# The last re/im swap of a long convolution: eight GpSimd copies in place of four DMAs, and the list order that goes with it

## The chip, the cores and the metric

One core of one Trainium2 chip. The metric is the device time of one launch in microseconds (us). The kernel before took 248.62 us in the median of two runs (248.44 and 248.81).

## What is computed

`x` has 2048 rows of 512 channels, in bfloat16. Two layers follow each other twice, with the same weights: a gated long convolution (A) and an MLP (B).

```python
# A: q = layernorm(x), k and v are given
k_shift = sum over t of 4 taps: k[s - 3 + t] * shift_k[:, 3 - t]
kv = k_shift * v
y  = irfft(rfft(kv padded to 2S) * rfft(ssm_k padded to 2S))[:S] + kv * ssm_D
x  = x + layernorm(x) * y
# B
h  = gelu(layernorm(layernorm(x)) @ w1 + b1)
x  = x + h @ w2 + b2
```

The convolution's result `y` depends on k, v, shift_k, ssm_k and ssm_D alone, and not on x. So it is computed once and used by both A layers.

## The kernel before, in words

**The convolution.** The 2048 time steps are cut into two halves of 1024. Each half is carried to the frequency side by matmuls with tables, and multiplied there. On the frequency side a number is complex. A tile is 128 partitions by 8192 columns, and a column group of 128 belongs to eight channels. The two groups of 64 partitions of a tile hold the two parts (re and im) of each number. One such group can be multiplied elementwise with another tile only as it lies; for the cross terms of a complex product a second copy of the tile is needed, with its two groups of 64 partitions swapped. That copy is the "swap" of this case.

The steps of one half, with their lines in the kernel before:

- `turn_h` (L563, matmuls at L571) turns the filter ssm_k. `turn_k` (L577, L589) and `taps` (L596, L609) make kv of the first half on TensorE, and `shift` (L703) makes that of the second half on VectorE.
- `stage1` (L617, matmuls at L630) and `stage2` (L635, matmuls at L644) transform it. Eight matmul groups of each make one tile. Each group of PSUM is moved to SBUF by `evac` (L539): an ACTIVATE on ScalarE (L544) or a copy on VectorE (L545), 128x1024 numbers at a time.
- The swaps: `swap_v` (L661) with pool=1 copies on GpSimd, 64 partitions at a time, viewed as 32-bit words (L667). The filter's first half is swapped so (C3 to C4), and the filter's second part too (C6 to C4). `swap` (L649) copies the second half's kv (C5 to C1) by four SBUF to SBUF DMAs of 512 KB, two issued by SyncE and two by ScalarE (through `dma`, L525).
- The products, elementwise on VectorE (`tt`, L534). Those of the second half, L870 and L871, go over four pieces g of 2048 columns: m = C5\*C3, C6 += m, then m = C1\*C3, C4 += m. The second pair needs the swapped tile C1.
- `inverse1` (L674, matmuls at L682, eight groups, two for each piece g) and `inverse2` (L688, L697) go back to time and give y.

**The MLP blocks.** Eight blocks of 512 rows (L962: `for L, b in ...`, counted k = 0 to 7): the A layer's norm and gating, then the layernorms, then the MLP. k = 0 to 3 use the first half's y, k = 4 to 7 the second half's. Statistics are VectorE's (L894 to L901), but the power -0.5 is GpSimd's (L902), and VectorE (L904) or ScalarE goes on with it. `norm` (L936) runs on ScalarE (L941) or VectorE (L942). The normed rows are transposed by DMA from SyncE's queue (L999), except in block 0 (on TensorE, L1007). The first MLP matmul is L1022, the gelu on ScalarE L1027, the second matmul L1042, and VectorE adds its result to x (L1046). A block is 44 matmuls of 512 columns at L1022 and 44 at L1042.

**What sets the order.** Nothing is run in the order in which it is written. Each operation is recorded with a cost and with what it reads and writes. `schedule` (L188) is a list scheduler: it walks over a model of the five engines, and picks for each engine the ready operation with the highest priority. The priority is the longest path behind an operation, plus a boost for its stage, plus an offset from a table that gives some operations, by number, a nudge (L1055). It also decides which engine, ScalarE or VectorE, empties a PSUM group, and which PSUM banks are used. `sync` (L320) sets the semaphore waits, and each engine then runs its list strictly in order. So a table entry can move any operation on any engine. A GpSimd operation waits in addition for the one before it on GpSimd.

Of the kernel before, what the change touches and what calls it, by code (L numbers as in the profile page):

```python
# [418 lines left out]
                getattr(block, e)(body)  # L419


WF, SPL, NA1, NDX, KP, KM, SG, PG, PSW, PLN, END, SPS, ST4, IA, SWA, PSH, BPE, TQ = 8, 1, 0, 64, 2, 0, 1, 1, 1, 0, 1, (0, 4), 0, 0, 0, 1, (), ()
S, D, FF = 2048, 512, 1376
B = 1024
EPS = 1e-5
# [39 lines left out]
def bass_interleave_layers__ssm_conv_h3__mixer_channel_mlp__prompt_kernel(  # L465
# [7 lines left out]
    def A(p0, n, off, *dims):  # L473
        return bass.AP(ar, p0 * AR + off, [[AR, n]] + [list(d) for d in dims])
# [16 lines left out]
    def place(n):  # L491
        o = pos[0]
        pos[0] += n
        return o
# [5 lines left out]
    C1, C3, C4, C5, C6 = (place(8192) for _ in range(5))  # L500
# [134 lines left out]
    def stage2(s, dst0, hf, g, dg0=0, nd=64, engs=None):  # L635

        tl = Tile(cv[hf], 0, hi[hf])
        nk = 1024 // nd
        ins = [(i, A(0, 128, R_S2 + (nk * g + i) * 128, [1, 128]), A(0, 128, s + (nk * g + i) * 64 + dg0, [1, nd]))
               for i in range(nk)]  # L640

        def f(e):
            for i, w, m in ins:
                r = e.matmul(Q(tl, 0, 128, i * nd, [1, nd]), w, m, start=True, stop=True)  # L644
            return r
        P.op(PE, f, nk * 29.0, reads=[x for y in ins for x in y[1:]], tile=tl, ni=2 * nk)
        evac(A(0, 128, dst0 + dg0 * 128 + nk * g, [128, nd], [1, nk]), lambda: Q(tl, 0, 128, 0, [1, nd], [nd, nk]), tl, engs)

    def swap(dst0, src0, dg0=0, nd=64):  # L649
        out = []  # L650
        for h in range(2):
            s = A(64 * h, 64, src0 + dg0 * 128, [1, nd * 128])
            out.append(dma(A(64 - 64 * h, 64, dst0 + dg0 * 128, [1, nd * 128]), s, nd * 37500, reads=[s], eng=(ACT if SWA else SP, ACT)[h]))
        return out

    def W32(p0, n, off, nd, nk):

        whole = bass.AP(ar, 0, [[AR, 128], [1, AR]]).bitcast(mybir.dt.int32)
        return bass.AP(whole.tensor, (p0 * AR + off) // 2, [[AR // 2, n], [64, nd], [1, nk // 2]] if nk < 128 else [[AR // 2, n], [1, nd * nk // 2]])

    def swap_v(dst0, src0, k0, nk, dg0=0, nd=64, pool=0):  # L661
        for h in range(2):
            i = A(64 * h, 64, src0 + dg0 * 128 + k0, [128, nd], [1, nk])
            o = A(64 - 64 * h, 64, dst0 + dg0 * 128 + k0, [128, nd], [1, nk])
            if pool:
                i2, o2 = W32(64 * h, 64, src0 + dg0 * 128 + k0, nd, nk), W32(64 - 64 * h, 64, dst0 + dg0 * 128 + k0, nd, nk)
                P.op(POOL, lambda e, i2=i2, o2=o2: e.tensor_copy(o2, i2), 1050.0, reads=[i], writes=[o])  # L667
            else:
                P.op(DVE, lambda e, i=i, o=o: e.tensor_copy(o, i), 710.0, reads=[i], writes=[o])
# [110 lines left out]
    for b in range(4):  # L780
        o, i = A(0, 128, R_DG + b * 512, [128, 4], [1, 128]), A(0, 128, R_ID, [0, 4], [1, 128])
# [73 lines left out]
            tt(o, A(0, 128, C5 + g, [1, n]), o, ALU.mult, 0.522 * n + 75.0)  # L855
    for g in range(8):
        stage2(C1, C5, 1, g)
    for i in range(2):
        swap(C1, C5, 32 * i, 32)
    if IA:  # L860
        for g in range(4):
# [101 lines left out]
    for L, b in [(0, 0), (0, 1), (1, 0), (1, 1), (0, 2), (0, 3), (1, 2), (1, 3)]:  # L963
# [89 lines left out]
                o = (b // 2) * B * 512 + (s % 8 - 1) * 512  # L1053
                outs.append(dma(dr(out, o, [8 * 512, 128], [1, 1024]), src, 1 << 18, reads=[src], writes=[]))
    P.schedule({  # L1055
        4: -2859500, 5: -2332800, 6: -1286000, 7: -1568900, 9: -2780000, 10: -3423500, 11: -4494400, 12: -7936200,
        13: -3456200, 14: -2083000, 15: -1086600, 17: -1246300, 18: -6727400, 49: 623300, 51: 1120500, 53: 397800,
        55: 878200, 57: 134800, 59: 357300, 61: 272900, 63: 442100, 65: 724800, 67: 1864700, 71: 1802700,
        73: 1680700, 75: 701900, 77: 2335500, 79: 3094300, 85: -855100, 87: -630300, 89: 139200, 122: -790700,
        140: 2949200, 142: 2930700, 148: 1114000, 149: -654400, 150: 2949300, 152: 2948900, 176: -1426600,  # L1060
        177: 1935700, 178: -1855200, 179: 1936500, 208: 1864200, 211: 1900900, 212: 2323700, 214: 1229900,
        215: 415700, 216: 1737900, 218: 2034800, 241: 274700, 252: -1863500, 254: -2126300, 261: 1300, 262: 1300,
        273: 692100, 274: 458400, 297: -395900, 323: -399300, 337: 1307700, 338: -581200, 371: 253000, 376: -62100,
        392: -327100, 404: -326700, 408: -517800, 419: -335200, 422: -237100, 430: -638000, 447: 389200, 448: 63500,
        449: -913400, 469: -1612800, 475: -1234900, 477: -724700, 481: -1965000, 483: -2062800, 485: -2047800,
        487: -1764900, 488: -752200, 495: -1158700, 500: -183700, 507: 501700, 508: -2594600, 525: -1427300,
        548: -4015000, 552: -130700, 564: -122800, 570: -595600, 572: -40300, 574: -359400, 576: -197300,
        580: -29700, 592: -1116400, 675: -2740700, 682: 2523700, 683: 850400, 772: -120300, 817: -3898900,
        819: -3017300, 821: -4122100, 823: -492500, 825: -4399400, 827: -4740300, 829: -3454600, 831: -2091700,
        833: -663100, 835: -1261600, 837: -1188500, 845: 1101200, 931: 187700, 1018: 1087200, 1019: 549100})  # L1070
    P.sync()
    P.emit(outs)

# [27 lines left out]
```

## Time and profile before

| what | value |
|---|---|
| two runs | 248.44 and 248.81 us, median 248.62 |
| the profiled execution | 248.81 us, of which the span is 246.8 us |
| granted TensorE clock | 1.00 |
| busy: TensorE, VectorE, ScalarE, GpSimd | 237.3, 185.0, 164.4, 49.7 us |
| TensorE's idle time with a cause, after the first 12 us | 5.2 us, the last of it at 118.7 us |
| GpSimd's swap copies (L667) | 16, median 1.037 us, longest 2.982 us |
| the four swap DMAs | 512 KB each, 7.5 us to landing (SyncE's), 8.9 us (ScalarE's) |
| last matmul group of `stage2` ends | 118.2 us |

Times in the views are microseconds from the start of the span. A row of the timeline gives start, length, engine, line, operation, operands, how often, and in brackets the idle time before it with what ended it. "PE" is TensorE, "DVE" VectorE, "ACT" ScalarE, "POOL" GpSimd; "SPq" and "ACTq" are the instruction queues of SyncE and ScalarE when they issue DMAs. Neighbouring equal instructions are merged in one row.

### The profile page before, as it was taken

What the parts mean: (1) busy time and instruction counts of PE and PEld (TensorE: products, weight loads), DVE (VectorE), ACT (ScalarE), POOL (GpSimd) and SP (SyncE); (2) the same over time, 40 slices, a digit from 0 to 9 for tenths busy, and PEclk for the clock granted to TensorE, in tenths of its full rate; (3) what the DMA queues carried; (4) which work ended last, traced back from release to release, by engine and by line L of the source; (5) the groups of instructions that cost most, each with busy time, mean ns of one, the idle gap of its engine ahead of it and who ended that gap; (6) DMA issues with size and microseconds to landing.
All of it is one profiled execution on the core that took longest, in us unless ns stands there. A gap on an engine that the chain in (4) does not pass through costs nothing.

```text
span 246.8 us, 5684 instructions
## 1 busy us (share of the span) xinstructions
PE 237.3 (96%) x2448; PEld 146.1 (59%) x2448; DVE 185.0 (75%) x353; ACT 164.4 (67%) x223; POOL 49.7 (20%) x48
## 2 busy tenths in 40 slices
PE   7999988899899999999899999999999999999995
PEld 4687778896687644455445647447844444444543
DVE  3579868999999998899989996699156866942012
ACT  3386779999999945868665589738914823733710
POOL 0000573000404396401304031122001111020000
PEclk9999999999999999999999999999999999999999
DMA  6999990613001440003590510033400030033002
GB/s 164 386 426 415 401 319 13 238 25 151 3 3 21 66 170 3 0 3 65 122 238 4 137 36 0 3 85 86 86 2 0 1 78 10 0 65 106 3 11 74
DMA packets 22097, 24.79 MB, mean 100 GB/s; under 512 B 15955, under 2 KB 17848, under 8 KB 20664
## 3 DMA queue, kind: packets, MB, share of 16 engines
q1 hardware_dynamic: 21752, 23.34, 30.5%
q10 hardware_dynamic: 320, 1.09, 1.9%
q8 instruction: 19, 0.31, 0.5%
q14 instruction: 6, 0.05, 0.1%
HBM read 16.56 MB, written 2.10 MB: 76 GB/s over the span
## 4 chain that ended last, share of the span: by engine, by line
PE 74%; ACT 14%; POOL 7%; DVE 2%; issue 1%; DMA 1%; POOLq 0%
PE ps L1042 28%; PE ps L1022 27%; ACT ar L544 12%; POOL ar L667 5%; PE ps L644 4%; PE ps L630 3%; PE ps L682 3%; PE ps L571 2%; POOL sm L902 2%; PE ps L609 1%; PE ps L697 1%; PE ps L768 1%; PE ps L762 1%; DMA ar<-ar 1%; DVE ar L534 1%
## 5 line engine op out<-in xcount | busy, mean ns | idle before, releaser
L544 ACT ACTIVATE ar<-ps 128x1024 bf16<-128x1024 f32 (+2 forms) x89 | 86.0, 1052 | 21.5 <-PE ps L630 8.6
L1027 ACT ACTIVATE ar<-ps,sm 128x512 bf16<-128x512 f32 (+3 forms) x110 | 63.5, 607 | 39.1 <-PE ps L1022 38.8
L534 DVE TENSOR_TENSOR ar<-ar 128x2048 bf16<-128x2048 bf16 (+2 forms) x76 | 77.9, 1054 | 5.1 <-ACT ar L544 2.8
L1022 PE MATMUL ps<-ar 128*128 128x512 bf16 (+3 forms) x440 | 80.9, 337 | 0.4 <-DMA ar<-ar 0.4
L1042 PE MATMUL ps<-ar 128*128 128x512 bf16 (+2 forms) x363 | 80.6, 373 | 0.3 <-ACT ar L1027 0.3
L1022 PEld LDWEIGHTS ps<-ar 128*128 128x128 bf16 (+1 forms) x440 | 42.9, 100 | 33.2 <-DMA ar<-ar 0.8
L1042 PEld LDWEIGHTS ps<-ar 128*128 128x128 bf16 (+1 forms) x363 | 34.6, 98 | 38.2 <-ACT ar L1027 0.9
L902 POOL TENSOR_TENSOR sm<-sm 128x2 f32<-128x2 f32 (+1 forms) x24 | 28.8, 1199 | 127.9 <-DVE sm L901 127.1
L1046 DVE TENSOR_TENSOR ar<-ar,ps 128x512 bf16<-128x512 bf16 (+1 forms) x33 | 21.6, 667 | 33.7 <-PE ps L1042 33.5
L894 DVE BATCH_NORM_STATS2 sm<-ar 128x6 f32<-128x512 bf16 x64 | 42.3, 683 | 0.3
L941 ACT ACTIVATE ar<-ar,sm 128x512 bf16<-128x512 bf16 x23 | 18.0, 808 | 9.1 <-DVE sm L904 5.6
L630 PE MATMUL ps<-ar 128*64 128x128 bf16 x640 | 22.1, 221 | 1.7 <-ACT ar L544 1.4
L667 POOL COPY ar<-ar 64x1024 int32<-64x1024 int32 x16 | 19.4, 1212 | 19.4 <-DVE ar L545 12.5
L630 PEld LDWEIGHTS ps<-ar 128*64 128x64 bf16 x640 | 18.5, 110 | 7.3 <-ACT ar L544 2.8
L644 PE MATMUL ps<-ar 128*128 128x64 bf16 x512 | 18.9, 193 | 2.9 <-ACT ar L544 1.3
L644 PEld LDWEIGHTS ps<-ar 128*128 128x128 bf16 x512 | 16.9, 98 | 6.6 <-ACT ar L544 3.1
L942 DVE TENSOR_SCALAR ar<-ar,sm 128x512 bf16<-128x512 bf16 x41 | 15.7, 410 | 1.6 <-POOL sm L902 1.1
L682 PEld LDWEIGHTS ps<-ar 128*128 128x128 bf16 x256 | 14.7, 98 | 1.4
L682 PE MATMUL ps<-ar 128*128 128x128 bf16 x256 | 15.5, 219 | 0.0
L545 DVE CAST ar<-ps 128x1024 bf16<-128x1024 f32 x9 | 10.8, 1219 | 2.4 <-PE ps L644 1.3
L896 DVE BATCH_NORM_AGGREGATE sm<-sm 128x2 f32<-128x6 f32 x64 | 10.3, 174 | 0.3
L904 DVE SCALAR_TENSOR_TENSOR sm<-sm 128x2 f32<-128x2 f32 (+1 forms) x21 | 3.6, 175 | 6.8 <-POOL sm L902 6.8
(33 smaller groups left out, 72.5 us busy)
## 6 DMA issues: line engine op xcount, KB each, us to landing
ar<-tab_s SPq DMA_DIRECT2D x4, 1024.0 KB, 18.1
ar<-in_A_ssm_k_dram SPq DMA_DIRECT2D x4, 512.0 KB, 6.9
ar<-in_A_q_dram SPq DMA_DIRECT2D x2, 1024.0 KB, 6.6
ar<-in_A_v_dram SPq DMA_DIRECT2D x2, 1024.0 KB, 8.9
out_dram<-ar SPq DMA_DIRECT2D x7, 256.0 KB, 2.4
ar<-in_A_k_dram SPq DMA_DIRECT2D x1, 1408.0 KB, 7.7
ar<-in_B_w_dram SPq DMA_DIRECT2D x1, 1376.0 KB, 22.1
ar<-in_B_w_dram SPq DMA_DIRECT2D x1, 1280.0 KB, 23.9
```

Of the source, the lines that this page charges most:

```text
L534: return P.op(eng, lambda e: e.tensor_tensor(o, a, b, op), dur, reads=[a, b], writes=[o])
L544: return e.activation(dst, src(), AF.Copy)
L630: r = e.matmul(Q(tl, 64 * ri, 64, i * 128, [1, 128]), w, m, start=j == 0, stop=j == len(terms) - 1)
L644: r = e.matmul(Q(tl, 0, 128, i * nd, [1, nd]), w, m, start=True, stop=True)
L667: P.op(POOL, lambda e, i2=i2, o2=o2: e.tensor_copy(o2, i2), 1050.0, reads=[i], writes=[o])
L682: r = e.matmul(Q(tl, 0, 128, i * 128, [1, 128]), w, m, start=j == 0, stop=j == len(pp) - 1)
L894: P.op(DVE, lambda e, st=st, x=x: e.bn_stats(st, x), 630.0, reads=[x], writes=[st])
L902: P.op(POOL, lambda e: e.tensor_tensor(r, v, h, ALU.pow), 1200.0, reads=[v, h], writes=[r])
L1022: r = e.matmul(Q(tl, 0, rows, 0, [1, nt]), w, m, start=dk == 0, stop=dk == 3)
L1027: P.op(ACT, lambda e, dst=dst, tl=tl, rows=rows, bias=bias, nt=nt: e.activation(dst, Q(tl, 0, rows, 0, [1, nt]), AF.Gelu_apprx_tanh, bias= ...
L1042: r = e.matmul(Q(tl, 0, 128, 0, [1, n]), ins[fc][0], ins[fc][1], start=fc == 0, stop=fc == 10)
L1046: P.op(DVE, lambda e, x=x, tl=tl, n=nc2: e.tensor_tensor(x, x, Q(tl, 0, 128, 0, [1, n]), ALU.add), 85.0 + nc2 * 1.055, reads=[x], writes=[ ...
```

## The change

Two things change. The second half's swap C5 to C1 is done by `swap_v` on GpSimd: four pieces of 2048 columns, two copies of 64 partitions each, in place of the four DMAs. And the table of offsets is another one: 126 entries in place of 112, on operations whose numbers behind the swap have moved by four.

```diff
-WF, SPL, ..., SWA, PSH, BPE, TQ = 8, 1, ..., 0, 1, (), ()
+WF, SPL, ..., SWA, PSH, BPE, TQ, PSX = 8, 1, ..., 0, 1, (), (), 1
...
     for g in range(8):
         stage2(C1, C5, 1, g)
-    for i in range(2):
+    for g in range(4 if PSX else 0):
+        swap_v(C1, C5, 0, 128, 16 * g, 16, pool=1)
+    for i in range(0 if PSX else 2):
         swap(C1, C5, 32 * i, 32)
...
     P.schedule({
-        4: -2859500, 5: -2332800, 6: -1286000, 7: -1568900, 9: -2780000, 10: -3423500, 11: -4494400, 12: -7936200,
...
+        4: -692700, 5: -476200, 6: -284700, 7: -137700, 9: -1381500, 10: -1285800, 13: -1222000, 14: -1491500,
...
```

Both kernels can be built, so the lists of all engines are known, though not their times. In the list after, the amount of work is the same on TensorE (2448 matmuls of the same shapes). These differences bear on what follows:

- Loads on SyncE: two of the four `stage2` tables go ahead of the load of v, the other two come right behind it, and the table of `inverse1` goes behind w1.
- In the first part (up to the second `turn_h`) VectorE empties 12 of the 32 large PSUM groups of `stage1` and `stage2` and not 9, and ScalarE 20 and not 23; of the eight smaller groups of `turn_k`, ScalarE empties six and not three. The first power on GpSimd stands ahead of the first-half copies and not behind six of them.
- Further on, four norms of block 2 stand together on ScalarE, where two were on ScalarE and two on VectorE.
- Behind the last `stage2` group TensorE has 44 matmuls of L1022 and 22 of L1042 (block 2) ahead of the first `inverse1` group, where it had 44 and 26; the eight `inverse1` groups and the four `inverse2` groups stand one by one between MLP matmuls, where some stood in pairs.
- GpSimd's list there is: one copy, the power of block 3's first norm, seven copies, the two powers of block 3's second norm.
- SyncE's two and ScalarE's two swap DMAs are gone from their lists.

## The prediction

> **What bounds the kernel now.** I read the page first, then TensorE's timeline, then the chain of waits, then the other engines' timelines where the chain leaves TensorE.
>
> ```profile
> span 246.8 us, 5684 instructions
> PE 237.3 (96%) x2448; PEld 146.1 (59%) x2448; DVE 185.0 (75%) x353; ACT 164.4 (67%) x223; POOL 49.7 (20%) x48
> ```
>
> TensorE is the bound, but not everywhere. Its timeline shows where it loses time; the last idle bracket of the whole run is this:
>
> ```profile
> 117.71 0.64 PE L644 MATMUL ps<-ar 128*128 128x64 bf16 x16 [0.31 <-DVE ar L1046]
> 118.74 6.42 PE L1022 MATMUL ps<-ar 128*128 128x512 bf16 x28 [0.39 <-DMA ar<-ar]
> ...
> 134.07 1.06 PE L682 MATMUL ps<-ar 128*128 128x128 bf16 x16
> ```
>
> From 118.74 to 244.12 us TensorE runs without a gap (44 matmuls of 512 columns in 9.51 us, 0.216 each). So whatever comes earlier ahead of the last L644 group (end 118.2, call it T) is won at the end, and whatever stalls TensorE behind T is lost. Between 42.3 and 70 us the chain lies on ScalarE (L544, 16.49 and 8.56 us), which empties PSUM without a pause while VectorE is full too. Ahead of that everyone waits for everyone:
>
> ```profile
> 26.99 6.52 POOL L667 COPY ar<-ar 64x1024 int32<-64x1024 int32 x6 [12.49 <-DVE ar L545]
> 33.60 2.10 POOL L902 TENSOR_TENSOR sm<-sm 128x4 f32<-128x4 f32 x2
> ...
> 34.65 0.41 DVE L942 TENSOR_SCALAR ar<-ar,sm 128x512 bf16<-128x512 bf16 x1 [1.06 <-POOL sm L902]
> ```
>
> A power (L902) stands behind six copies, and VectorE behind the power. The swap that is replaced, and what VectorE does beside it:
>
> ```profile
> 119.44 1.18 SPq L525 DMA_DIRECT2D ar<-ar  x2
> ...
> 119.82 2.07 ACTq L525 DMA_DIRECT2D ar<-ar  x2
> 121.94 2.42 ACT L1027 ACTIVATE ar<-ps,sm 128x512 bf16<-128x512 f32 x4 [1.44 <-PE ps L1022]
> ...
> 125.09 0.69 DVE L534 TENSOR_TENSOR ar<-ar 128x1024 bf16<-128x1024 bf16 x1 [1.00 <-ACT ar L941]
> ...
> 130.76 1.20 DVE L534 TENSOR_TENSOR ar<-ar 128x2048 bf16<-128x2048 bf16 x1
> 132.00 1.22 DVE L534 TENSOR_TENSOR ar<-ar 128x2048 bf16<-128x2048 bf16 x1
> ```
>
> Last, how copies and products treat each other, from the chain and VectorE's timeline (a copy alone takes 1.04):
>
> ```profile
> 91.07 2.43 DVE L534 TENSOR_TENSOR ar<-ar 128x4096 bf16<-128x4096 bf16 x1
> ...
> 91.42 2.99 POOL ar L667
> 94.46 1.04 POOL ar L667
> ```
>
> The copy that starts under a product makes no headway until the product ends (2.99 = 1.04 + 1.95). The product that starts 0.29 ahead of the end of the copy before it takes 2.43 and not 2.29; another (85.83, 1.33 and not 1.22) lost 0.11 under 0.26 of a copy.
>
> **The change, step by step.** All sums are against the profiled execution (248.81 us, span 246.8); the median is 0.19 below it, and I carry the differences over to 248.62.
>
> 1. Up to 42 us: the list. I followed the lists after by hand from 12.4 us, with 0.91 for a large emptying on ScalarE back to back, 1.14 on VectorE, 0.6 for L894, 1.85 for a `taps` group, 0.5 for an L630 or L644 group, 1.04 a copy. ScalarE sheds three large groups and takes three small ones (3 x 0.91 - 3 x 0.53 = 1.1 less), VectorE takes 2.3 more but no longer waits 1.06 for the power, which goes ahead of the copies. Emptying of the second `turn_h` then starts at about 40.4 (42.26 before), the products on VectorE at 40.25 (42.24): -1.9. Bounds: 0, if a load is late, and -2.2, the two gains on their own (1.1 + 1.06). The loads moved on SyncE: 2 MB of `stage2` tables pass v, which at 410 GB/s puts v some 5 us later, by bytes at about 19.4; VectorE first needs it at 23. The `inverse1` table lands by 30, needed after 40. Both cost nothing, and would if TensorE's taps were 3 us earlier.
>
> 2. 42 us to T: same operations, ScalarE and VectorE full in both, so the lead is carried. One piece is given back: block 2's four norms stand on ScalarE (4 x 0.72 = 2.9) ahead of two gelus that free L1042, and wait for a power that stands under a 4096 product, as it did before (2.98 at 99.08 against 1.01 alone). Before, it was two norms, and TensorE lost 0.27. By hand TensorE loses up to 1.9 there; what it loses is taken from a queue that had slack, so I take +0.6, bounds 0 and +1.9. T then comes 1.3 early.
>
> 3. The DMAs removed: 1.18 us of SyncE's queue (its next transposes are not due until 134), 1.44 us of ScalarE, and with that the 1.00 that VectorE waits for ScalarE at 125.09. The landing itself is hidden: 8.9 us behind 119.8 is 128.7, and VectorE, full with block 3's norm, first uses C1 at 130.76.
>
> 4. The copies added: 8 x 1.04 = 8.3 us on a GpSimd that is busy 4.7 us between 120 and 140. As work they are hidden: the last piece is due some 24 us behind T. But VectorE sets the time of the first L682 group. From the emptying of the last L644 group (T + 1.3) it needed 119.70 to 133.14 = 13.4 us before, 1.0 of it waiting; the same operations after, less one norm, are 11.9, done at T + 13.2. TensorE arrives at T + 66 x 0.216 = 14.3, where it arrived at 15.9 before. So there is 1.1 us of slack (0.9 before), and none of this work can be delayed beyond it. In this stretch VectorE runs nearly only products and norms from SBUF. Two prices: a product that starts under a copy lost 0.14 of 0.29 and 0.11 of 0.26, that is 0.45 us for each us, so 8 x 1.04 x 0.45 = 3.8; and the power of block 3's first norm is queued behind the first copy, with VectorE's L904 behind it and four norms, gating and statistics behind that: 0 to 0.95, I take 0.4. Sum 3.8 + 0.4 - 1.1 = +3.1 on TensorE. Bounds: 0, if copies slip in under statistics and only they wait, as in the 2.99 row; and 8 x (1.04 - 0.15) + 0.95 - 1.1 = +7.0, if every product waits out a whole copy but for 0.15 (0.29 - 0.14) of it. The value is the ratio that two rows show, between both ends.
>
> The Trainium skill, SBUF — State Buffer, section "Who interferes with whom", says that an elementwise VectorE operation with both inputs in SBUF and a GpSimd operation that reads SBUF exclude each other: the first to start holds the shared port for its whole length. For the copy under a product this trace agrees (2.99 against 1.04); for a product under a copy it shows half of it (0.14 of 0.29). By the rule alone the sum of this step would be 8.3 + 0.4 - 1.1 = +7.6 and the time 254.9.
>
> 5. Behind that: the later pieces have 0.1 to 0.9 us of slack against their L682 groups, and go late with the first, at no further cost. `inverse2` one group at a time: from the end of its first group to block 4's first L1022 there were 13.0 us (154.6 to 167.57), of which the chain of gating, statistics, power, norm and transpose took 11.0 (landing at 165.6). After there are 12.1. No cost; up to +1 if VectorE is late by more. The tail (244.14 to 246.8: last add and its store) is the same.
>
> Sum: -1.9 + 0.6 + 3.1 = +1.8, so 248.62 + 1.8 = 250.4 us.
>
> **Rivals.**
> - *The copies hide* (the other side: faster). GpSimd gets its time under L894 and L1046 operations, which left copies at 1.04 between 88 and 91 us, and VectorE loses less than its slack of 1.1 us. For it: six of the eight copies at 85 to 97 cost VectorE nothing. Against it: there VectorE ran mostly such operations, here mostly products. It decides at 1.1 us: below that step 4 is 0, and the time 248.62 - 1.3 = 247.3.
> - *Full alternation.* Copy and product take turns and each product waits out a copy: +7.0, so 248.62 - 1.3 + 7.0 = 254.3. For it: powers that come under back to back products get in at the first boundary (at 142.12, 1.96 and not 1.01). Against it: the two rows with half the price.
> - *The lead of the first 42 us is not there*, because the list waits elsewhere (v, or banks), and the copies cost what I say: 250.4 + 1.9 = 252.3.
>
> **How the numbers follow.** Forecast 0.45 (its own range 248.8 to 252), copies hidden 0.30, full alternation 0.15, no lead 0.10. The range leaves out the half of the first rival beyond 246.8 and most of the alternation beyond 253.4: 246.8 to 253.4. 2% is 5 us, about what a measurement of this kernel can tell from no change: above 253.6 lies most of the full alternation and a little of "no lead", 0.13; below 243.6 the lead would have to be 5 us, more than twice its bound, 0.02; between 0.85.
>
> **What would show it.** Right: no SBUF to SBUF DMA, the products starting near 40 us, T near 117, eight copies behind T of which several take 2 us and more, products of 2048 above 1.22 beside them, and TensorE idle ahead of the first L682 by about 3 us with VectorE as the cause. Wrong: the first L682 without a wait (copies hidden), a wait of 6 us and more (alternation), the products starting at 42 or later (no lead), or a new wait ahead of the second gelu of block 1 or of block 4's first L1022.

## The result, and the profile after

The changed kernel took 256.78 us (256.56 to 257.0), the kernel before 248.62: a ratio of 1.0328 (1.0278 to 1.0378), 8.2 us slower. The profiled execution is the one of 257.0 us. First its page:

```profile
span 255.2 us, 5688 instructions
PE 238.6 (94%) x2448; PEld 147.0 (58%) x2448; DVE 193.2 (76%) x347; ACT 168.3 (66%) x229; POOL 56.7 (22%) x56
PEclk9799999999999999999998699999999999999999
PE 62%; DVE 17%; ACT 14%; POOL 3%; issue 2%; DMA 1%; ACTq 0%; POOLq 0%
```

VectorE's busy time grew by 8.2 us with six instructions fewer, VectorE's part of the chain of waits went from 2% to 17%, and the row of TensorE's clock, all nines before, has two slices near 140 us at 8 and 6 tenths (and one at 7 near 8 us, which the last section takes up). TensorE's timeline shows the place:

```profile
117.60 1.27 PE L644 MATMUL ps<-ar 128*128 128x64 bf16 x32
119.98 9.75 PE L1024 MATMUL ps<-ar 128*128 128x512 bf16 x44 [1.11 <-DMA ar<-ar]
129.57 4.92 PE L1044 MATMUL ps<-ar 128*128 128x512 bf16 x22
139.04 1.89 PE L682 MATMUL ps<-ar 128*128 128x128 bf16 x16 [4.56 <-DVE ar L534]
140.72 4.74 PE L1044 MATMUL ps<-ar 128*128 128x512 bf16 x12
145.30 1.06 PE L682 MATMUL ps<-ar 128*128 128x128 bf16 x16
```

The first L682 waits 4.56 us for a product, where it did not wait before. And behind the wait TensorE is slow: 16 matmuls of 128 columns take 1.89 and not 1.06, 12 of 512 columns take 4.74, where 12 at full clock take 2.75. The windows over this stretch (columns: length; busy time of TensorE, of its weight load, VectorE, ScalarE, GpSimd; granted clock; DMA) give the reason:

```profile
136.00:138.00 2.00, 0.00 (x0) 0.00 (x0) 2.00 (x8) 1.08 (x2) 0.19 (x1) 0.98 0.02 4
138.00:140.00 2.00, 0.96 (x10) 0.96 (x11) 2.00 (x5) 0.23 (x1) 1.65 (x2) 0.50 0.00 0
142.00:144.00 2.00, 2.00 (x6) 0.76 (x5) 2.00 (x3) 2.00 (x4) 0.00 (x0) 0.50 0.76 209
146.00:148.00 2.00, 2.00 (x20) 1.17 (x18) 0.32 (x2) 1.60 (x2) 0.00 (x0) 1.00 0.32 66
```

While TensorE waits its granted clock falls to a half, and it stays there until 144.8, nearly 6 us into work. Last, the two engines that shut each other out. GpSimd's timeline in stretches of 1 us (four of the eight copies), then VectorE's:

```profile
124.37 1.04 POOL L667 COPY ar<-ar 64x1024 int32<-64x1024 int32 x1
125.46 1.92 POOL L667 COPY ar<-ar 64x1024 int32<-64x1024 int32 x1
128.54 1.58 POOL L667 COPY ar<-ar 64x1024 int32<-64x1024 int32 x1
130.19 1.91 POOL L667 COPY ar<-ar 64x1024 int32<-64x1024 int32 x1
```

```profile
124.42 2.07 DVE L534 TENSOR_TENSOR ar<-ar 128x2048 bf16<-128x2048 bf16 x1
126.41 1.13 DVE L944 TENSOR_SCALAR ar<-ar,sm 128x512 bf16<-128x512 bf16 x1
127.45 1.18 DVE L944 TENSOR_SCALAR ar<-ar,sm 128x512 bf16<-128x512 bf16 x1
128.55 0.68 DVE L534 TENSOR_TENSOR ar<-ar 128x1024 bf16<-128x1024 bf16 x1
129.15 2.05 DVE L534 TENSOR_TENSOR ar<-ar 128x2048 bf16<-128x2048 bf16 x1
134.01 0.68 DVE L896 BATCH_NORM_STATS2 sm<-ar 128x6 f32<-128x512 bf16 x1
```

Read them together. The copy of 124.37 is first and runs alone; the product of 124.42 waits for its end, 2.07 and not 1.22. The next copy (125.46) waits for that product, 1.92; the norm of 126.41 waits for that copy, 1.13 and not 0.36. They take turns. Two rows are untouched: the product of 128.55, which got in ahead of the copy recorded at 128.54 (that copy took 1.58, the rest of the product and its own 1.04), and the statistics of 134.01, which ran beside the last copy.

How the 8.4 us between the ends of the last L1042 or L1044 (244.10 and 252.54) come together, stretch by stretch of TensorE's timeline:

| stretch | before | after | difference |
|---|---|---|---|
| to the first L630 | 12.43 | 12.54 | +0.1 |
| to the second `turn_h` (L571) | 28.59 | 28.57 | 0.0 |
| to the end of the last L644 | 77.33 | 77.76 | +0.4 |
| wait ahead of the next L1022 / L1024 | 0.39 | 1.11 | +0.7 |
| wait ahead of the first L682 | 0 | 4.56 | +4.6 |
| slow matmuls behind it | 0 | 2.8 | +2.8 |
| rest of the work behind the last L644 | 125.36 | 125.22 | -0.1 |

(The 2.8 is the time from the first L682 to the end, 113.50, less 110.72 in the kernel of the first experiment, which has the same list and no wait there. It belongs to this execution: the other one, 0.44 us faster, has a mean granted clock of 0.993 over its span where this one has 0.980.)

### The profile page after: what moved, and what is told of

It reads as the page before. It is cut to its first block, busy times and chain, and to the rows that moved or that the text cites. A ratio compares the mean times of both kernels' runs of the same rounds, so it can differ in the third digit from the quotient of the medians.

```text
span 255.2 us, 5688 instructions
## 1 busy us (share of the span) xinstructions
PE 238.6 (94%) x2448; PEld 147.0 (58%) x2448; DVE 193.2 (76%) x347; ACT 168.3 (66%) x229; POOL 56.7 (22%) x56
## 4 chain that ended last, share of the span: by engine, by line
PE 62%; DVE 17%; ACT 14%; POOL 3%; issue 2%; DMA 1%; ACTq 0%; POOLq 0%
PE ps L1044 26%; PE ps L1024 22%; ACT ar L544 12%; DVE ar L534 5%; DVE sm L896 4%; PE ps L682 3%; PE ps L630 3%; POOL sm L904 2%; DVE ar L944 2%; PE ps L644 2%; PE ps L571 2%; DVE ar L614 2%; DVE ar L545 1%; DMA ar<-in_A_ssm_D_dram 1%; PE ps L697 1%
## 5 line engine op out<-in xcount | busy, mean ns | idle before, releaser
L544 ACT ACTIVATE ar<-ps 128x1024 bf16<-128x1024 f32 (+2 forms) x89 | 85.1, 1033 | 26.6 <-PE ps L630 8.7
L534 DVE TENSOR_TENSOR ar<-ar 128x2048 bf16<-128x2048 bf16 (+2 forms) x76 | 81.4, 1110 | 6.8 <-ACT ar L544 6.5
L1044 PE MATMUL ps<-ar 128*128 128x512 bf16 (+2 forms) x363 | 83.0, 379 | 0.4 <-ACT ar L1029 0.4
L1024 PE MATMUL ps<-ar 128*128 128x512 bf16 (+3 forms) x440 | 80.2, 337 | 1.1 <-DMA ar<-ar 1.1
L1024 PEld LDWEIGHTS ps<-ar 128*128 128x128 bf16 (+1 forms) x440 | 42.9, 100 | 32.9 <-DMA ar<-ar 1.2
L1044 PEld LDWEIGHTS ps<-ar 128*128 128x128 bf16 (+1 forms) x363 | 35.2, 99 | 39.4 <-issue 2.6
L904 POOL TENSOR_TENSOR sm<-sm 128x2 f32<-128x2 f32 (+1 forms) x24 | 26.2, 1091 | 130.1 <-DVE sm L903 128.9
L1048 DVE TENSOR_TENSOR ar<-ar,ps 128x512 bf16<-128x512 bf16 (+1 forms) x33 | 21.6, 666 | 35.1 <-PE ps L1044 35.1
L667 POOL COPY ar<-ar 64x1024 int32<-64x1024 int32 x24 | 29.1, 1211 | 22.0 <-DVE ar L534 12.0
L943 ACT ACTIVATE ar<-ar,sm 128x512 bf16<-128x512 bf16 x29 | 22.6, 806 | 14.7 <-DVE sm L906 7.1
L630 PE MATMUL ps<-ar 128*64 128x128 bf16 x640 | 22.1, 221 | 2.9 <-ACT ar L544 1.4
L630 PEld LDWEIGHTS ps<-ar 128*64 128x64 bf16 x640 | 18.5, 110 | 8.4 <-issue 3.2
L682 PE MATMUL ps<-ar 128*128 128x128 bf16 x256 | 16.8, 225 | 4.6 <-DVE ar L534 4.6
L644 PE MATMUL ps<-ar 128*128 128x64 bf16 x512 | 18.4, 193 | 2.3 <-ACT ar L544 1.7
L644 PEld LDWEIGHTS ps<-ar 128*128 128x128 bf16 x512 | 16.8, 98 | 5.4 <-ACT ar L544 3.2
L682 PEld LDWEIGHTS ps<-ar 128*128 128x128 bf16 x256 | 15.6, 101 | 6.9 <-DVE ar L534 5.1
L944 DVE TENSOR_SCALAR ar<-ar,sm 128x512 bf16<-128x512 bf16 x35 | 16.5, 499 | 0.9 <-DMA ar<-ar 0.6
L545 DVE CAST ar<-ps 128x1024 bf16<-128x1024 f32 x12 | 14.5, 1219 | 2.0 <-PE ps L630 1.1
L906 DVE SCALAR_TENSOR_TENSOR sm<-sm 128x2 f32<-128x2 f32 (+1 forms) x21 | 3.7, 178 | 6.9 <-POOL sm L904 6.8
```

The source lines that it names most:

```text
L534: return P.op(eng, lambda e: e.tensor_tensor(o, a, b, op), dur, reads=[a, b], writes=[o])
L544: return e.activation(dst, src(), AF.Copy)
L630: r = e.matmul(Q(tl, 64 * ri, 64, i * 128, [1, 128]), w, m, start=j == 0, stop=j == len(terms) - 1)
L682: r = e.matmul(Q(tl, 0, 128, i * 128, [1, 128]), w, m, start=j == 0, stop=j == len(pp) - 1)
L904: P.op(POOL, lambda e: e.tensor_tensor(r, v, h, ALU.pow), 1200.0, reads=[v, h], writes=[r])
L943: return e.activation(o, x, AF.Identity, bias=mr[2], scale=mr[1])
```

## The experiments

Theory: copies and VectorE's products exclude each other, so TensorE waits, and the wait costs the clock besides. Rivals: the new list makes VectorE late by itself; the clock fell for another reason. Numbers such as 285 are operations in the order in which the program makes them: 285 to 292 are the new copies, 607 the power of the fourth block's first norm, 293 to 308 the products. Each edit stands between the planner and the waits: an operation is moved in an engine's finished list or given another predecessor, and everything else stays where it was. "Ratio" is to the kernel before, run beside it.

**1. Copies cut short.**

```
-        swap_v(C1, C5, 0, 128, 16 * g, 16, pool=1)
+        swap_v(C1, C5, 0, 128, 16 * g, 16, pool=1, part=1)   # 64 words, not 1024
```

> The kernel after, with each of the eight new copies cut to one sixteenth of its columns (64 words of a partition instead of 1024); order, waits and all else are kept. It leaves 15/16 of that swap out, so the products read words that were not swapped. Theory (copies and VectorE's products lock each other out, and the idle TensorE then loses its clock): the 4.6 us wait ahead of the first L682 and the 2.6 us lost at the lower clock behind it both go, 256.8 - 7.2 = 249.6 us, within 0.6. Rival 1 (VectorE is late by its new list, not by the copies): the wait stays, 255 us or more. Rival 2 (the lower clock at 140 to 150 us has nothing to do with the wait): 4.6 less only, 252.2 us, with a dip of the clock still there.

Measured: 248.49 us, ratio 1.0004 (0.9984 to 1.0025). VectorE's and GpSimd's timelines:

```profile
126.12 3.02 DVE L534 TENSOR_TENSOR ar<-ar 128x1024 bf16<-128x1024 bf16 x4
```

```profile
124.23 6.49 POOL L667 COPY ar<-ar 64x64 int32<-64x64 int32 x7
```

The seven short copies still take 0.93 each, waiting under products, but four products now take 3.02 where they took 5.54. TensorE does not wait ahead of L682, and the clock stays at 1.0. So the loss goes with the length of the copies, all of it by the ratio, and the lower clock goes with the wait. The median is 1.1 below the theory's number, which had added the 0.4 and 0.7 ahead of L682 and allowed 0.6. The profile, of the slowest of the ten executions (250.03), shows both; what balances them in the median is not shown, and the start, which scatters by 2 us among all profiles, hides it.

**2. The new list with the old DMAs.**

```
     c = P.ops[285:293]                      # eight copies -> four DMAs
+    put(c[2], SP, 557); put(c[6], SP, 287)  # behind SyncE's transposes
+    put(c[3], ACT, 559); put(c[7], ACT, 288)
```

> The kernel after, its lists kept on every engine, but with the second half's swap by the four DMAs of the kernel before (two behind SyncE's transposes, two on ScalarE behind its first gelu of the block). Theory: what is left is the list alone, which is 0.5 us late at the last L644 group and 0.7 us more at the L1024 behind it: 249.6 us, up to 0.5 more for the issues on ScalarE; no wait ahead of the first L682, clock 1.0. Rival 1 (the new list is what costs): 254 us or more.

Measured: 250.30 us, ratio 1.0087 (1.0047 to 1.0127). The list does not cost 8 us. Part of its 1.6 is the price of a list that was made for copies: the first product of C1 stands at 125 us, VectorE waits 1.86 for the DMA there, and L682 waits 0.63, where the theory had no wait.

**3. The old list with copies.**

```
+    at = 603                     # block 3's power
     for g, h, x in copies:       # eight copies in place of the four DMAs
+        put(x, POOL, at); at = x.i
```

> The kernel before, its lists kept, but with its four SBUF to SBUF DMAs replaced by the eight copies on GpSimd, put behind the power that starts at 119.9 us. Theory: VectorE loses about a whole copy for each copy, 8 x 1.04 = 8.3, less 0.9 of slack and 1.0 of the wait for ScalarE's delayed norm: TensorE waits some 6.4 us ahead of its first L682, and loses some 2.6 us by the clock behind it: 257.6 us, within 1.5. Rival 1 (the new list is what costs): 248.6 to 250 us. My forecast's price (0.45 us for each us): 8 x 1.04 x 0.45 - 1.9 = 1.8, 250.4 us, with no dip of the clock.

Measured: 250.69 us, ratio 1.0070 (1.0046 to 1.0095). A miss by 7 us, and the most useful one. The copies cost VectorE 4.1 us here: the norms' L904 (1.00 and not 0.16), three L942 (0.7 to 0.75 each), two products (0.83 together) and one more (0.25). The last copies ran beside four statistics and delayed none of them. 4.1 less the 1.9 of slack is the wait seen in TensorE's timeline; the windows show the clock:

```profile
135.24 1.07 PE L682 MATMUL ps<-ar 128*128 128x128 bf16 x16 [2.24 <-DVE ar L534]
```

```profile
136.00:138.00 2.00, 2.00 (x12) 0.82 (x10) 2.00 (x3) 2.00 (x3) 0.00 (x0) 0.62 0.03 6
138.00:140.00 2.00, 2.00 (x7) 0.71 (x6) 1.47 (x3) 1.02 (x2) 0.00 (x0) 0.53 0.61 125
```

2.24 and 1.5 of slow matmuls make 3.7; the median is only 2.0 above the kernel before. This execution's first L630 was 1.0 earlier (11.43) than in the profile of before, and the others were up to 1.0 faster than it (250.25 to 251.23). The fastest of the four (250.25) has a granted clock of 1.000 over its span and the others 0.993, so the slow stretch was not there every time; whether the wait was, is not seen. The forecast's price, 0.45 us for each us, gave 250.4 here and would pass by the number: 4.1 for 8.35 us of copies is 0.49. The rows show no such price: what stands behind a copy loses 0.7 to 0.85 or the copy's tail, and statistics lose nothing. What follows: a copy has no price of its own. It depends on what VectorE has next.

**4. The power first.**

```
+    q = P.order[POOL]
+    q.remove(P.ops[607]); q.insert(q.index(P.ops[285]), P.ops[607])
```

> The kernel after with one change of GpSimd's order: the power of the fourth block's first norm goes ahead of the first of the eight copies instead of behind it. Theory: the power's delay is a small part (VectorE waited 0.9 us for it at 124.3), the eight copies still lock out VectorE: 0.5 to 1.5 us less, 255.3 to 256.3 us. If the power in between the copies is the main cause: 4 us less or more, 252 us.

Measured: 255.26 us, ratio 1.0253 (1.0227 to 1.0279), 1.5 below the kernel after, at the end of what the theory allowed. The wait ahead of L682 is 3.70 and not 4.56.

**5. A wait of TensorE without any copy.**

```
+    again(P.ops[291], 5)        # kernel before: the product issued six times
```

> The kernel before (swap by DMA), with the first product of C1 (the 2048-column VectorE product at 130.8 us, two ahead of the first L682) issued five times more into the same place. It makes TensorE wait there with no copy on GpSimd: 5 x 1.2 = 6.0 less 0.9 of slack = 5.1 us of wait. Theory (a wait of some us costs the clock behind it, whatever the reason of the wait): the matmuls behind the first L682 run at a lower granted clock, some 2.8 us lost, as in the kernel after: 248.7 + 5.1 + 2.8 = 256.6 us. Rival (the lower clock came with the copies, or by chance): 253.8 us, clock 1.0.

Measured: 257.07 us, ratio 1.0322 (1.0280 to 1.0364). TensorE's timeline and the windows:

```profile
141.16 1.89 PE L682 MATMUL ps<-ar 128*128 128x128 bf16 x16 [5.36 <-DVE ar L534]
142.84 4.60 PE L1042 MATMUL ps<-ar 128*128 128x512 bf16 x14
```

```profile
140.00:142.00 2.00, 0.84 (x9) 0.85 (x10) 2.00 (x5) 0.20 (x1) 1.65 (x1) 0.50 0.00 0
142.00:144.00 2.00, 2.00 (x13) 1.28 (x12) 2.00 (x3) 2.00 (x4) 0.00 (x0) 0.50 0.07 15
```

The same 1.89 for the first L682 and the same half clock, with the swap by DMA; from the first L682 to the end it is 112.23 us and not the 110.03 of the kernel before, so 2.2 are lost. The copies are not needed for it: a wait of TensorE for VectorE's products alone brings the lower clock.

**6. The order of the first loads,** once taken back in the kernel after (here), once put into the kernel before (13).

```
+    P.order[SP][:4] = [P.ops[i] for i in (8, 16, 6, 7)]
```

> The kernel after with SyncE's first four loads in the order of the kernel before (the 128 KB table ahead of the small bias, and the two ssm_k halves the other way round). In four profiles with the order of the kernel after L774 waited 0.6 to 0.9 us for in_A_ssm_D, in two with the order of before it did not. Theory: the order makes the wait; it goes, and the first L630 comes 0.5 to 0.8 earlier, but L1024 and L682 behind the last L644 wait as they did: 256.8 - 0.7 = 256.1 us. Rival (chance of the run, or a wait that is made up by 42 us): 256.8 us.

Measured: 255.61 us, ratio 1.0278 (1.0254 to 1.0301), 1.2 below the kernel after and 0.5 below the theory. In its profile L774 does not wait, and the first L630 starts at 11.36, in that of the kernel after at 12.54; both waits behind the last L644 are still there (1.15 and 4.55).

**7. The copies spread.**

```
+    new = (607, 285, 286, 287, 288, 622, 629, 289, 290, 291, 292)   # GpSimd's order
+    P.ops[287].preds[616] = "raw"                # held until the last product ahead of the statistics
```

> The kernel after with the eight copies spread: the power of the fourth block's first norm ahead of the first copy, two copies (group 0) where they were, two (group 1) held until the last VectorE product ahead of the four statistics has ended, four (groups 2 and 3) behind the two powers of the next norms. Theory (a copy costs VectorE 0.7 to 0.85 us where a product or a norm is next, and nothing under statistics): 1.55 for group 0, nothing for group 1, both against 1.0 of slack; groups 2 and 3 cost 3.2 behind the first L682, against 1.2 of slack. TensorE waits 0.5 ahead of the first L682 and some 1 to 2 us behind it, and the clock loses under 0.5: 250 to 251 us. Rival (each copy costs the same wherever it stands, as the price comes from their number): 255 us or more.

Measured: 253.88 us, ratio 1.0210 (1.0159 to 1.0260): 2.9 better than the kernel after, not 6. GpSimd's timeline, then VectorE's, then TensorE's:

```profile
129.83 2.14 POOL L667 COPY ar<-ar 64x1024 int32<-64x1024 int32 x2 [6.00 <-DVE ar L534]
135.79 6.97 POOL L667 COPY ar<-ar 64x1024 int32<-64x1024 int32 x4
```

```profile
129.80 1.29 DVE L896 BATCH_NORM_STATS2 sm<-ar 128x6 f32<-128x512 bf16 x2
135.84 8.00 DVE L534 TENSOR_TENSOR ar<-ar 128x2048 bf16<-128x2048 bf16 x4
```

```profile
133.68 1.06 PE L682 MATMUL ps<-ar 128*128 128x128 bf16 x16
144.50 1.89 PE L682 MATMUL ps<-ar 128*128 128x128 bf16 x16 [2.76 <-DVE ar L1048]
```

The part that the theory priced came out: two copies under two statistics run unhindered (1.07 each) and delay nothing, the first L682 does not wait, and four copies among four products cost 3.4 (8.00 against 4.62). What I had wrong was the slack of the later groups: not 1.2 but 0.3, so the loss came back one group later as waits of 0.30 and 2.76 and 1.7 of slow clock.

**8. Copies twice.**

```
+    for o in P.ops[285:293]:
+        again(o)
```

> The kernel after with each of the eight copies issued twice into the same place. Theory: eight more exclusions of about 0.8 us, 6 to 8 us more of VectorE's time ahead of the first L682; the wait of 4.6 becomes 10 to 12 us, and the clock loses about as much again as in the kernel after (2.6 to 4 us): 263 to 266 us. Price of my forecast (0.45 us for each us of copy): 3.8 more, 260.6 us. If the copies hid: 256.8 us.

Measured: 260.96 us, ratio 1.0501 (1.0480 to 1.0521): 4.2 above the kernel after, below the 6 to 9 I gave. It is what my forecast's price gave (260.6), but by luck: by that price the products ahead of L682 would lose 3.8 more, and the rows show 0.7 of that (the product at 139.14 took 1.91 and not 1.19). VectorE's products and norms take the same 2.07, 2.23 and 5.53 as with single copies. With the copies back to back, each product that is issued waits for one copy and no more, so twice the copies do not find twice the products. What grew is the waiting for GpSimd's queue, in which the norms' powers stand behind the copies; VectorE's timeline:

```profile
146.13 0.16 DVE L906 SCALAR_TENSOR_TENSOR sm<-sm 128x2 f32<-128x2 f32 x1 [4.48 <-POOL sm L904]
```

**9. VectorE relieved ahead of 42 us.**

```
+    P.order[DVE].remove(P.ops[123]); put(P.ops[123], ACT, 104)   # an L545 becomes an L544
+    # norms 350, 351 behind 448 in VectorE's list
```

> The kernel after, with VectorE relieved between 25 and 33 us: one large emptying (an L545 at 25.9) goes to ScalarE, and the two slow norms at 31.6 (L944, 1.37 together) go behind the second power's L906. Theory for the lead that did not come (VectorE, with the norms and statistics drawn forward onto it, became what bounds 23 to 38 us): the L614 that frees the L630 at 34.2 ends 1.1 earlier, the wait of 0.97 there goes, and the products start 0.5 to 1.1 earlier: 256.8 - 0.8 = 256.0 us; the stretch from the first L630 to the second turn_h's L571 is 27.5 to 28.1 us and not 28.57. Rival (the stretch is set by TensorE's or the loads' own time): 28.57 again, 256.8 us.

Measured: 256.65 us, ratio 1.0330 (1.0300 to 1.0360), and 28.65 us from the first L630 to the second `turn_h`: the theory fails. VectorE now stands idle 1.85 us ahead of an L614, and TensorE waits at another place:

```profile
29.33 0.64 PE L630 MATMUL ps<-ar 128*64 128x128 bf16 x16 [1.15 <-ACT ar L544]
```

**10. The copies at VectorE's harmless operations.**

```
+    new = (607, 285, 286, 287, 288, 289, 622, 629, 290, 291, 292)
+    # product 617 goes right behind product 616 in VectorE's list, ahead of the statistics
+    for i, p in ((287, 616), (290, 299), (291, 303), (292, 302)):   # an L1048 follows 299, 303, 302
+        P.ops[i].preds[p] = "raw"
```

> The kernel after with the copies put where VectorE runs operations that were not delayed by a copy: two behind the power (as in the spread before), three held for the four statistics, which are put in one row, and each of the last three held until a product ends that has an L1048 (one operand from PSUM) behind it. Theory: a copy costs nothing under statistics, and only what it sticks out of an L1048 (1.04 - 0.6 = 0.4): 1.2 us behind the first L682 in place of the 3.4 that four copies cost in the spread before, of which 2.2 less, and 1 us less of clock: 253.9 - 3 = 251 us, 250 to 252. Rival (L1048 is delayed as products are): 253 to 254 us.

Measured: 251.20 us, ratio 1.0115 (1.0085 to 1.0146), as expected. Three copies beside the statistics (1.25 for two statistics, as ever) cost only a small L903 0.45; the four products take 5.47 where the earlier spread had 8.00:

```profile
131.58 1.25 DVE L896 BATCH_NORM_STATS2 sm<-ar 128x6 f32<-128x512 bf16 x2
137.97 5.47 DVE L534 TENSOR_TENSOR ar<-ar 128x2048 bf16<-128x2048 bf16 x4
143.36 0.68 DVE L1048 TENSOR_TENSOR ar<-ar,ps 128x512 bf16<-128x512 bf16 x1
```

So 2.7 us are left to the kernel before, and some 5.5 of the 8.2 come back by moving eight copies, one power and one product. The L1048 of 143.36 has a copy beside it (143.50) and keeps its 0.68.

**11 and 12. The edits together,** with copies and with DMAs.

```
     # 6 + 9 + 10
     # 6 + 9, and four DMAs, all on SyncE; product 295 behind the statistics
```

> The last two edits together, and SyncE's first four loads in the order of the kernel before (1.0 to 1.2 less when it was changed alone): 251 - 0.8 - 1.1 = 249 us, 248 to 250.5. It would stand level with the kernel before, with all swaps on GpSimd.

> The new list with the loads' order of before and VectorE relieved as above, and the second half's swap of x by four DMAs again, all issued by SyncE, the first product of C1 put behind the statistics so that it does not wait for them. Theory: the copies' whole price goes (248.5 with copies cut to a sixteenth), then 1.1 for the loads and 0.8 for VectorE: 246.6 us, 246 to 247.5, faster than both kernels. Rival (the lead is eaten behind 42 us): 248 us or more.

Measured: 250.81 us, ratio 1.0094 (1.0073 to 1.0114), and 248.87 us, ratio 1.0013 (0.9999 to 1.0028). Both miss the theory by about 2: from the first L630 (11.2 us, early) to the second `turn_h` they need 29.4 to 29.6 us and not 28.57. Edit 9 harms there, and it was left out of the last one.

**13. The order of the loads, in the kernel before.**

```
+    P.order[SP][:4] = [P.ops[i] for i in (16, 8, 7, 6)]
```

> The kernel before with one change: SyncE's first four loads in the order of the kernel after (the small bias ahead of the 128 KB table, the two ssm_k halves the other way round). L774 waited for in_A_ssm_D in all eight profiles with that order (0.3 to 1.3 us) and in one of six with the order of before. Theory: the order costs what it gave when it was taken back in the kernel after (256.8 to 255.6): 248.5 + 1.0 = 249.5 us. Rival (the start scatters by 2 us between executions whatever the order, and the wait is made up later): 248.5 us, within 0.3.

Measured: 248.97 us, ratio 1.0023 (1.0005 to 1.0042): some 0.6 us by the ratio (0.1 to 1.0), 0.2 between the two medians. L774 waited 1.07 in its profile. It lies between theory and rival: the order costs something, less than the 1.2 of experiment 6.

**14. The new list without the copies and without edit 9.**

> The new list with the first four loads in the order of the kernel before and the second half's swap of x by four DMAs, all on SyncE, with the first product of C1 behind the statistics; without the edit that relieved VectorE (which only put another wait in the place of the one it took, and brought the second turn_h 0.8 later in the two kernels with the early start). Theory: 248.87 - 0.8 = 248.1 us, within 0.4, a little under the kernel before at best: without the copies' price the new list is worth at most half a microsecond. If the list were worth the 1.9 us of my forecast: 246.6 us.

Measured: 248.17 us, ratio 0.9971 (0.9947 to 0.9994). It is the one version that beats both kernels, by 0.7 us (0.2 to 1.3) against the one before: so much the list is worth with the old order of the loads, and not 1.9.

## Why the prediction was wrong

The forecast was 250.4 us, and the time is 6.4 above it. The difference goes step by step.

1. *Step 1, the lead of 1.9: it did not come* (28.57 against 28.59 us). I followed VectorE, ScalarE and GpSimd by hand and never asked how much TensorE could gain at all. Its timeline in this stretch shows four waits before:

```profile
26.46 1.71 PE L644 MATMUL ps<-ar 128*128 128x64 bf16 x48 [0.28 <-ACT ar L544]
33.64 1.08 PE L630 MATMUL ps<-ar 128*64 128x128 bf16 x32 [0.30 <-DVE ar L614]
36.25 2.01 PE L644 MATMUL ps<-ar 128*128 128x64 bf16 x62 [0.48 <-DVE ar L545]
39.00 2.10 PE L644 MATMUL ps<-ar 128*128 128x64 bf16 x66 [0.74 <-issue]
```

and after:

```profile
26.02 1.57 PE L644 MATMUL ps<-ar 128*128 128x64 bf16 x48 [0.23 <-DVE ar L614]
34.20 1.08 PE L630 MATMUL ps<-ar 128*64 128x128 bf16 x32 [0.97 <-DVE ar L614]
```

They are 1.8 us together before; after, with two of 0.23 besides, 1.7. A lead of 1.9 would have needed every one of them gone. The waits for VectorE's emptyings and for the end of the stage went, and a longer wait for an L614, which the norms drawn forward delay, took their place. Experiment 9 took that one away and got another of 1.15.

2. *Step 2, the norms on ScalarE: right in the sum (+0.4 for +0.6), mostly by luck.* At the gelu behind the norms, the place that I had named, TensorE waits 0.36 where it waited 0.27. A wait for VectorE that I had not seen is larger, and other waits of this stretch became shorter or longer. TensorE's timeline after:

```profile
93.32 0.64 PE L630 MATMUL ps<-ar 128*64 128x128 bf16 x16 [0.55 <-DVE ar L1048]
106.33 1.90 PE L1044 MATMUL ps<-ar 128*128 128x512 bf16 x8 [0.36 <-ACT ar L1029]
```

The further 0.7 ahead of the next L1024, a wait for the transposes, was not in it; that wait varied from 0.39 to 1.18 among the kernels with this list.

3. *Step 3 and the slack: right.* No SBUF to SBUF DMA is left, and without the copies' weight VectorE is done 1.1 us before TensorE arrives (experiment 1: 133.71 against 134.83), the slack that I had worked out. That the two agree to a tenth is chance: in experiment 1 TensorE comes later by 1.12 of waiting for the transposes, and VectorE by 0.90 of waiting for the power, and neither was in my 1.1.

4. *Step 4, the price of a copy: this step failed; it was mis-sized.* I had two rows in which a product lost "0.14 of 0.29 and 0.11 of 0.26" and read them as a ratio, 0.45 us for each us. They were an offset: a product loses what is left of the copy less some 0.15, and both rows had caught only the tail of one. A copy that starts in the gap behind a product has its full length left, and the next product loses 0.72 to 0.85. VectorE's stretch ahead of L682 grew from 12.89 (experiment 1) to 18.67 us, 5.8 for 8.35 us of copies; the wait is 4.56 where I had 3.1. I had also counted products only: two L944 lost 0.8 each. The power cost more than its 0.4, too: VectorE waits 0.90 for it (at 124.34), and with the power ahead of the copies (experiment 4) the wait was shorter by 0.86. The bound that I gave as full alternation, copies at 0.89 each, had the mechanism; I took the ratio and gave the bound a chance of 0.15.

The Trainium skill, SBUF — State Buffer, section "Who interferes with whom", had this right where I weighed it against the two rows: whoever issues first holds the shared port for its whole instruction. The same section sets apart an operation with at most one input in SBUF outside the two-port modes, and counts `tensor_scalar` among those that can take the port. This case agrees on each: L944 1.13 and not 0.36, statistics and L1048 0.68 beside a copy as without one. By the rule alone the forecast's sum would have been 254.9 us, nearer than mine, but by errors that cancel: it has 7.6 of waiting where 4.56 came, and has neither the missing lead nor the clock.

5. *A step that was missing: the clock.* I priced 3.1 us of waiting as 3.1 us. Behind its first matmul TensorE never stood still for longer than 1.0 us in the profile of before, so no row showed what a wait does; the alternative "full alternation" lacked it too, and so ended at 254.3. It cost 2.8 in the profiled execution (experiment 5: 2.2 without a copy). The Trainium skill, TensorE: Matmul & The Clock Gate, Part 1, tells of a gate that halves the clock when the array was idle for a window of about 3.4 us; I had not drawn on it, though my own sum had TensorE idle for 3.1 us.

Sum: 1.9 for step 1, 1.5 for step 4, 2.8 for the clock, 0.7 for the transposes, 0.1 for the start, less 0.2 for step 2 and 0.1 for the rest of the list, make 6.7, against 6.6 between the two profiles (8.4 less the forecast's 1.8) and 6.4 between the medians. Of the three alternatives two came true at once, and I had added each to the forecast alone: the missing lead in full, and the alternation in its mechanism, with 4.56 of its 7.0 us of waiting.

Open: how often the clock falls at all behind a wait of this length (the last section), how much of the start is the loads' order (1.2 in one pair of kernels, 0.6 in the other, with a scatter of 11.2 to 13.6 us for the first L630), and what bounds the stretch to 42 us, where taking away one wait only showed the next.

## What to carry to other kernels

A small loss in a row is the loss for that overlap: before it becomes a price, see how much of the other instruction was left, and what the price is when all of it is left. Work on GpSimd is put beside VectorE's statistics and its reads from PSUM, not beside products and norms; moved like that, the same eight copies cost 2.7 us and not 8.2. And a gain ahead of the bound engine is at most the idle time of that engine there, while a new wait on it can be dearer than its length.

## What the runs showed of the hardware

- TensorE's granted clock fell to 0.50 some 2.2 to 5.1 us after the matmuls stopped ahead of an L682 (experiments 7 and 8; 3.4 in the kernel after), and stayed there for about 3.4 us (experiments 3, 4, 7, 8 and 9) or 6.8 us (the kernel after, experiments 5 and 6). A wait of 2.24 us was enough in experiment 3, and the fall then came 1.2 us after the matmuls had resumed (135.24, and the clock at 0.50 from 136.4). The window of about 3.4 us of the Trainium skill, TensorE: Matmul & The Clock Gate, Part 1, agrees with the two lengths; that the array has to be idle for a whole window does not agree with the 2.24 us.
- It is not tied to such a wait alone. The fastest executions of experiments 3 and 7 have a clock of 1.000 over the whole span, though how long TensorE waited in them was not seen. And three profiles have one more stretch of 3.4 us at 0.50, from about 8 us (the kernel after 8.2 to 11.6, experiments 8 and 14 about 7.9 to 11.3), though behind its first matmul TensorE had stood still there for 0.79, 1.33 and 0.32 us at the longest. What lowered it there is open; no time is seen to be lost by it (L571's 32 matmuls took 3.46 us in the kernel after and 3.62 at full clock in the kernel before).
- With the same wait of 4.56 us the slow clock cost 2.8 us in one kernel and 1.4 in another (experiment 9), by whether it lasted two such lengths or one.
- Small operations pay in full: an L906 on 128 x 4 words took 0.99 and not 0.15 behind a copy (experiment 4).
- A copy of 64 words takes 0.93 when it stands under products: on GpSimd it is nearly as long as a copy of 1024 that runs alone (1.04), and the products lose next to nothing (experiment 1: 1.27 and not 1.22 for one of 128x2048).
